# The last ten pairs of heads of an attention stage, taken four heads at a time: chunks of 128 keys and one 64x64-tile step for the keys left over

## The chip, the core and the metric

The kernel runs on one core of a Trainium2 chip. TensorE (PE) multiplies, VectorE (DVE), ScalarE (ACT) and GpSimd (POOL) do the elementwise work, and SyncE (SP) issues nearly all DMAs. The metric is the device time of one execution in microseconds (us), as the median of several runs; less is better.

## What is computed

Three stages in fp32. Sigmoid attention for 4 batches of 12 heads (448 keys and queries, head size 64), a gated product with w_a, w_b and w_out on its 1792 rows, and a soft mixture of 8 experts:

```python
def _attn_ref(q, k, v):                      # (4, 12, 448, 64)
    scores = scale * np.matmul(q, k.transpose(0, 1, 3, 2)) - np.log(S)
    attn = 1.0 / (1.0 + np.exp(-scores))
    return np.matmul(attn, v)

x = attn_out.transpose(0, 2, 1, 3).reshape(B * S, H * D)
x = (x @ w_a) * (x @ w_b) @ w_out            # 768 -> 1536 -> 768
logits = x @ phi                             # 32 slots, softmax over tokens and over slots
slot_out[e] = np.maximum(slot_input[e] @ w1[e], 0) @ w2[e]
out = c @ slot_out
```

## The kernel before

The attention goes by pairs of heads, numbered g = 0 to 23 (six pairs in a batch, the two heads of a pair on partitions 0 to 63 and 64 to 127). For one pair:

- `load_qkv` loads k and q as four DMAs each and v as one DMA, all on SP's queue. For pairs 13 to 23 k and q arrive in blocks of 32 that VectorE transposes in place (`transposed`), and `split_heads` makes a rounded fp32r part (`kh`, `qh`) and a rest (`kl`, `ql`) of each. Two buffers hold each of these, three each of the loads.
- `emit_S` makes the scores in four chunks of 112 keys. A chunk is three fp32r products (kh·qh, kl·qh, kh·ql) for each head; the two heads have different rows of the array and run side by side. ScalarE's sigmoid takes each chunk of 112x448 from PSUM to a tile `a`.
- `emit_PV` multiplies the `a` tiles with v in full fp32: four chunks, the two heads in different columns of the array, side by side, both into one PSUM tile. `emit_x` copies that on ScalarE to the tile that the next stage reads, frees v, and asks for the v of the pair three further on.

`att` is a generator that fixes the order. In the step of pair g, from pair 12 on, it writes: transposes and split of pair g+1; the first chunk of scores of g; PV and x of pair g-1; the other chunks of g. The caller takes a step of it and then a step of other work: `operands` and `prep_u`, which prepare the next stage (POOL subtractions, rounding casts `S2h` and `wx` on VectorE that wait for POOL), and the group and logits work of batch 0 (`first_LG`). After the last scores the first product of `unit(0)` (banks `ab`) is issued, then PV and x of pair 23, then the rest of `unit(0)`, which goes on with `late_operands` that need the last x.

A load waits on SP for its buffer, and whatever stands behind it on SP waits too. PSUM has tags `sc` (4 buffers), `ms` (2) and `ab` (2). The end of the kernel streams the experts' weights through buffers that come free as earlier stages end.

Of the kernel before, what the change touches and what calls it, by code (L numbers as in the profile page):

```python
# [9 lines left out]
F32 = mybir.dt.float32  # L10
# [25 lines left out]
def body(ctx, tc, q, k, v, w_a, w_b, w_out, phi, w1, w2, out):  # L36
# [81 lines left out]
    qkv_t = {}  # L118
    held = []

    def load_qkv(g, names):
# [6 lines left out]
        for src, nm, n in ((k, "k", 3), (q, "q", 3), (v, "v", 3)):  # L128
            if nm not in names:
                continue  # L130

            if g >= GT0:
                if nm == "v":
                    t = atp.tile([T, 2, C, D], F32, tag="vn", name="vn", bufs=n)
                    sp.dma_start(out=t, in_=src[b, 2 * p:2 * p + 2].rearrange("h (c p) d -> p h c d", c=C))
                else:
                    t = atp.tile([128, 2 * C * D], F32, tag=nm + "n", name=nm + "n", bufs=n)
                    t = t[:, :S].rearrange("p (n d) -> p n d", d=32)
                    for j in range(4):
                        sp.dma_start(out=t[32 * j:32 * j + 32],  # L140
                                     in_=src[b, 2 * p + j // 2][:, j % 2 * 32:j % 2 * 32 + 32].rearrange(
                                         "(n t) d -> t n d", t=32))
                qkv_t[nm, g] = t
                continue
            s = src[b, 2 * p:2 * p + 2].rearrange(
                "h (c p) d -> p h c d" if nm == "q" else "h (p c) d -> p h c d", c=C)
            if nm == "v":
                t = atp.tile([T, 2, C, D], F32, tag="vn", name="vn", bufs=n)
                sp.dma_start(out=t, in_=s)
            else:  # L150
                t = atp.tile([128, 2 * C * D], F32, tag=nm + "n", name=nm + "n", bufs=n)
# [5 lines left out]
    stk = {}  # L157
# [21 lines left out]
    def emit_TK(g):  # L179
        if g >= B * NP:  # L180
            return
        if g >= GT0:
            for nm in "kq":
                split_heads(g, nm, transposed(g, nm), dve.tensor_copy)
                load_qkv(g + 3, nm)
            return
        tk = transposed(g, "k")
        if not g:
            tq = transposed(g, "q")
        split_heads(g, "k", tk, dve.tensor_copy)  # L190
        if not g:
            split_heads(g, "q", tq, act.copy)
# [8 lines left out]
    def emit_S(g, chunks):  # L201

        (kh, kl), (qh, ql) = stk[g]["k"], stk[g]["q"]
        for c in chunks:
            ab = (g < NP or g > 2 * NP) and c == 2
            sc = [ms((T, S)) if g >= GT0 and c == 0 and not h else ps_tile("ab" if ab else "sc", [T, S], 2 if ab else 4)
                  for h in range(2)]
            cs = slice(c * T, (c + 1) * T)
            for i, (kx, qx) in enumerate(((kh, qh), (kl, qh), (kh, ql))):
                for h in range(2):  # L210
                    r = slice(64 * h, 64 * h + 64)
                    pe.matmul(sc[h], kx[r, cs], qx[r], start=(i == 0), stop=(i == 2))  # L212
            for h in range(2):
                a = atp.tile([T, S], F32, tag="a", name="a", bufs=11)
                act.activation(a, sc[h], AF.Sigmoid, bias=nlog[:T], scale=1.0 / math.sqrt(D))  # L215
                a_t[g, h, c] = a

    pv_t = {}

    def emit_PV(g, cs):  # L220
        if cs[0] == 0:
            pv_t[g] = ps_tile("sc", [128, S], 4) if g < 2 * NP else ms()
        for c in cs:
            for h in range(2):
                pe.matmul(pv_t[g][64 * h:64 * h + 64], qkv_t["v", g][:, h, c, :], a_t.pop((g, h, c)),  # L225
                          start=(c == 0), stop=(c == C - 1))

    xt = {}

# [12 lines left out]
    def emit_x(g):  # L242
        pv = pv_t.pop(g)
        qkv_t.pop(("v", g))
        b, kk = divmod(g, NP)
        if b:
            xt[g] = raw_x(b, kk)
            act.copy(xt[g], pv)
        else:
            xh = x0p.tile([128, S], F32R, tag=f"xh{kk}", name=f"xh{kk}")  # L250
            xl = x0p.tile([128, S], F32R, tag=f"xl{kk}", name=f"xl{kk}")
            act.activation(xh, pv, AF.Copy)
            dve.tensor_tensor(xl, pv, xh.bitcast(F32), op=ALU.subtract)
            xt[g] = (xh, xl)
        load_qkv(g + 3, "v")

    def att():
# [483 lines left out]
    def unit(u):  # L741
# [520 lines left out]
```

## Time and profile before

| | |
|---|---|
| median of 3 runs (lowest to highest) | 674.41 us (674.21 to 678.49) |
| the profiled execution | 674.89 us, its span 673.1 us |
| TensorE busy | 635.7 us, 94% |
| VectorE, ScalarE, POOL busy | 390.6, 290.8, 309.5 us |
| TensorE's granted clock, mean | 0.989 of full speed |

The span runs from the first instruction to the last; the 1.8 us around it belong to the time as well. Busy shares are averages over stages with different limits. Pairs 14 to 23 lie between 226 and 292 us of the span.

### The profile page before, as it was taken

How to read it: one execution, taken by the hardware profiler on the slowest of the kernel's cores; microseconds unless marked ns; L12 is line 12 of the kernel's file. 1: busy time of each engine (PE TensorE's matmuls, PEld its weight loads, DVE VectorE, ACT ScalarE, POOL GpSimd, SP SyncE). 2: the span in 40 equal slices, each digit the busy share in tenths (PEclk: the TensorE clock that was granted, in tenths of full speed). 3: DMA queues.
4: the chain of work that ended last, by engine and by line, in shares of the span. 5: the costliest groups of instructions: out<-in, count | busy, mean ns of one | idle time of the engine just before them, and what ended most of it. 6: DMA issues, size and time to landing. Idle time of an engine off the chain costs nothing.

```text
span 673.1 us, 10911 instructions
## 1 busy us (share of the span) xinstructions
PE 635.7 (94%) x4035; PEld 451.7 (67%) x4035; DVE 390.6 (58%) x563; ACT 290.8 (43%) x527; POOL 309.5 (46%) x236
## 2 busy tenths in 40 slices
PE   6999999999998899999999999999999998997685
PEld 4456777777765455569989898898879896442131
DVE  4675898999973769657876777754233322200013
ACT  4888778779645588763432223201110002110022
POOL 0233677686745239558996585742344442000000
PEclk9999999999999999999999999999999999999788
DMA  9997999998868977201123233341999999999998
GB/s 211 272 247 215 288 291 335 287 296 265 259 151 203 247 126 134 64 2 47 48 89 95 70 93 99 97 126 44 305 384 344 407 357 339 405 415 416 411 374 307
DMA packets 150356, 154.25 MB, mean 229 GB/s; under 512 B 81856, under 2 KB 126752, under 8 KB 147232
## 3 DMA queue, kind: packets, MB, share of 16 engines
q1 hardware_dynamic: 143728, 150.00, 71.9%
q10 hardware_dynamic: 6576, 3.56, 1.8%
q8 instruction: 32, 0.52, 0.3%
q14 instruction: 20, 0.16, 0.1%
HBM read 126.36 MB, written 27.17 MB: 228 GB/s over the span
## 4 chain that ended last, share of the span: by engine, by line
PE 80%; DMA 12%; ACT 2%; DVE 2%; SPq 1%; issue 1%; ACTq 1%; POOL 0%; POOLq 0%; DVEq 0%
PE ab L578 26%; PE sc L761 15%; DMA e<-in_moe_w 8%; PE ab L761 8%; PE sc L212 7%; PE sc L225 5%; PE ms L225 5%; PE ms L174 2%; PE ms L854 2%; PE ab L212 2%; DMA gkp<-in_moe_w 1%; PE ms L501 1%; PE ms L400 1%; PE ms L212 1%; SPq L140 1%
## 5 line engine op out<-in xcount | busy, mean ns | idle before, releaser
L375 POOL TENSOR_TENSOR w<-gk,cy 128x768 int32<-128x768 int32 x36 | 66.1, 1837 | 91.7 <-DVE gk L370 53.7
L215 ACT ACTIVATE a<-sc,sums 112x448 f32<-112x448 f32 x147 | 84.3, 642 | 14.2 <-PE sc L212 14.1
L578 PE MATMUL ab<-t,wh 128*128 128x448 f32 x288 | 65.1, 371 | 0.0
L578 PEld LDWEIGHTS ab<-t,wh 128*128 128x128 f32 x288 | 53.4, 188 | 6.1 <-issue 1.3
L471 POOL TENSOR_TENSOR wl<-wr,wh 128x768 fp32r<-128x768 f32 x16 | 29.5, 1841 | 49.8 <-DVE wh L470 26.0
L585 ACT COPY misc<-ab 128x448 f32<-128x448 f32 x24 | 12.9, 537 | 83.3 <-PE ab L578 76.4
L471 POOL TENSOR_TENSOR wl<-w,wh 128x768 fp32r<-128x768 f32 x24 | 46.6, 1942 | 2.5 <-ACT wh L470 2.5
L1188 PE MATMUL ab<-e,gk 128*32 128x384 f32 x240 | 33.6, 567 | 10.1 <-DMA e<-in_moe_w 10.1
L588 DVE TENSOR_TENSOR misc<-misc,ab 128x448 f32<-128x448 f32 x24 | 14.7, 614 | 44.1 <-PE ab L578 44.1
L225 PE MATMUL sc<-a,vn 112*64 112x448 f32 x192 | 39.1, 546 | 1.0 <-ACT a L215 1.0
L225 PE MATMUL ms<-a,vn 112*64 112x448 f32 x192 | 38.7, 546 | 1.1 <-ACT a L215 1.1
L368 DVE TENSOR_SCALAR mf<-gk 128x768 f32<-128x768 f32 x36 | 33.8, 940 | 8.3 <-ACT gk L357 8.3
L212 PE MATMUL sc<-qh,kh 64*112 64x448 f32 x147 | 34.5, 421 | 0.7 <-ACT qh L162 0.6
L578 PE MATMUL ab<-xh,wl 128*128 128x448 f32 x144 | 34.3, 374 | 0.9 <-POOL wl L471 0.9
L369 DVE TENSOR_SCALAR gk<-mf 128x768 uint32<-128x768 uint32 x36 | 34.3, 953 | 1.2
L578 PE MATMUL ab<-xh,wh 128*128 128x448 f32 x144 | 34.9, 378 | 0.0
L641 ACT CAST wx<-T 128x384 fp32r<-128x384 f32 x21 | 10.8, 513 | 55.6 <-DVE T L663 40.0
L578 PE MATMUL ab<-xl,wh 128*128 128x448 f32 x144 | 34.5, 375 | 0.0
L642 POOL TENSOR_TENSOR wx<-wr,wx 128x384 fp32r<-128x384 f32 x29 | 32.8, 1133 | 3.5 <-ACT wx L641 3.4
L578 PE MATMUL ab<-t,wl 128*128 128x448 f32 x144 | 34.3, 373 | 0.0
L642 POOL TENSOR_TENSOR wx<-T,wx 128x384 fp32r<-128x384 f32 x23 | 24.6, 1068 | 19.8 <-ACT wx L641 18.5
L1235 DVE COPY o<-sc 128x384 f32<-128x384 f32 x10 | 5.4, 555 | 48.0 <-PE sc L1214 46.8
(465 smaller groups left out, 1494.5 us busy)
## 6 DMA issues: line engine op xcount, KB each, us to landing
e<-in_moe_w SPq DMA_DIRECT2D x23, 1024.0 KB, 8.4
e<-in_moe_w SPq DMA_DIRECT2D x23, 768.0 KB, 15.0
wr<-ab SPq DMA_DIRECT2D x14, 768.0 KB, 4.5
ab<-w SPq DMA_DIRECT2D x24, 384.0 KB, 7.1
vn<-in_v SPq DMA_DIRECT2D x24, 224.0 KB, 4.5
gk<-gk SPq DMA_DIRECT2D x24, 224.0 KB, 4.2
e<-in_moe_w SPq DMA_DIRECT2D x14, 384.0 KB, 8.8
wr_cv<-in_moe_w_a SPq DMA_DIRECT2D x6, 768.0 KB, 6.5
```

The lines of the kernel that those rows point to most:

```text
L212: pe.matmul(sc[h], kx[r, cs], qx[r], start=(i == 0), stop=(i == 2))
L215: act.activation(a, sc[h], AF.Sigmoid, bias=nlog[:T], scale=1.0 / math.sqrt(D))
L225: pe.matmul(pv_t[g][64 * h:64 * h + 64], qkv_t["v", g][:, h, c, :], a_t.pop((g, h, c)), start=(c == 0), stop=(c == C - 1))
L368: dve.tensor_scalar(mf, m, LOW, HIGH, op0=ALU.max, op1=ALU.min)
L369: dve.tensor_scalar(mi, mf.bitcast(U32), 3, 0x3FFFFFFF, op0=ALU.logical_shift_left, op1=ALU.bitwise_and)
L375: pool.tensor_tensor(thirds(w), m.bitcast(I32), thirds(cy_t.pop(x)), op=ALU.add)
L471: pool.tensor_tensor(wl, t, wh.bitcast(F32), op=ALU.subtract)
L578: pe.matmul(t, w[:, kk * 128:(kk + 1) * 128], xt[b * NP + kk][xi], start=(s == 0 and kk == 0), stop=(s == 2 and kk == KD - 1))
L588: dve.tensor_tensor(g, g, t, op=ALU.mult)
L642: pool.tensor_tensor(w[:, 1], t, w[:, 0].bitcast(F32), op=ALU.subtract)
L761: pe.matmul(t, w[:, wi, k * 128:(k + 1) * 128], xs[ORDER[m], k][xi], start=(s == 0 and k == 0), stop=(s == 2 and k == 2))
L1188: pe.matmul(sps[h][32 * j:32 * j + 32], hT[:, 2 * x + i, 2 * j + g], ring[order2[n + j]][0][:, i, c0:c0 + w], start=(g == 0 and x == 0 and ...
```

## The change

From pair 14 on (`GQ`) two pairs make a group of four heads n to n+3: the even pair holds heads n and n+3, the odd pair n+2 and n+1. Each pair does three chunks of 128 keys. The 64 keys that are left of each of the four heads are done once per group, at the odd pair: `emit_S_rest` has four fp32 products of 64 rows by 64 columns, one in each quarter of the array, and two sigmoids of 128x448; the odd pair's PV ends with four such products of 64x64 more. PV of a group goes to two `ab` tiles, and both x copies come after the odd pair's PV, one on ScalarE and one on VectorE. q stays in its buffer until `emit_S_rest` (four buffers), and the 64 k columns are copied to `kr`. v comes in four DMAs instead of one. The first product of `unit(0)` and the logits of batch 0 use other banks, and one step of `rest_LG` is later.

The diff, without what only moves lines:

```diff
+GQ = 2 * NP + 2
+    def heads(g):
+        n = 2 * (g % NP)
+        return (n, n + 1) if g < GQ else (n, n + 3) if g % 2 == 0 else (n, n - 1)
...
+                else:
+                    t = t.rearrange("p (c d) -> p c d", d=D)
+                    for h in range(2):
+                        sp.dma_start(out=t[:, 3 * h:3 * h + 3],
+                                     in_=src[b, hs[h]][:384].rearrange("(c p) d -> p c d", c=3))
+                    rest = (hs[0], hs[0] + 2) if g % 2 == 0 else (hs[1], hs[1] + 2)
+                    for h in range(2):
+                        sp.dma_start(out=t[64 * h:64 * h + 64, 6], in_=src[b, rest[h]][384:])
...
-                split_heads(g, nm, transposed(g, nm), dve.tensor_copy)
-                load_qkv(g + 3, nm)
+                t = transposed(g, nm)
+                split_heads(g, nm, t, dve.tensor_copy)
+                if g >= GQ:
+                    if nm == "k":
+                        kr = atp.tile([128, 64], F32, tag="kr", name="kr", bufs=3)
+                        dve.tensor_copy(kr, t[:, 384:])
+                        t = kr
+                    whole[nm, g] = t
+                if nm == "k" or g <= GQ:
+                    load_qkv(g + 3, nm)
...
+    def emit_S_rest(g):
+        sc = [ms() for _ in range(2)]
+        for d in range(2):
+            for h in range(2):
+                r, f = slice(64 * h, 64 * h + 64), 64 * (d ^ h)
+                pe.matmul(sc[h][f:f + 64], whole["k", g - 1 + d][r], whole["q", g - 1 + d][r], start=True, stop=True)
+        for h in range(2):
+            sigmoid(g, h, 3, sc[h], 128)
+        for d in range(2):
+            del whole["k", g - 1 + d], whole["q", g - 1 + d]
+            load_qkv(g + 3 + d, "q")
...
+        for c in range(3):
+            for h in range(2):
+                pe.matmul(pv[h ^ odd][64 * h:64 * h + 64], qkv_t["v", g][:, 3 * h + c], a_t.pop((g, h, c)),
+                          start=(c == 0), stop=False)
+        if odd:
+            a = [a_t.pop((g, h, 3)) for h in range(2)]
+            for r in range(2):
+                for h in range(2):
+                    s = slice(64 * r, 64 * r + 64)
+                    pe.matmul(pv[r][64 * h:64 * h + 64], qkv_t["v", g - 1 + h][s, 6], a[h][s], start=False, stop=True)
...
-            act.copy(xt[g], pv)
+            (dve.tensor_copy if g > GQ and g % 2 else act.copy)(xt[g], pv)
...
-                emit_PV(g - 1, (0, 1, 2, 3))
-                emit_x(g - 1)
+                emit_PV(g - 1)
+                if g <= GQ:
+                    emit_x(g - 1)
+                elif g % 2 == 0:
+                    emit_x(g - 2)
+                    emit_x(g - 1)
...
+                if g >= GQ and g % 2:
+                    emit_S_rest(g)
+                    yield 800
...
-            tag = UBANK[(7 * u + m) % 6]
+            tag = UBANK[(7 * u + m) % 6] if u + m else "sc"
...
-        lf = ms()
+        lf = ms() if b else ps_tile("ab", [128, S], 2)
...
-        for _ in range(4 if b == 1 else 1):
+        for _ in range((3, 4, 1)[b]):
```

Where it moves instructions. On TensorE, before, the last chunk of scores of pair 15 and the PV of pair 14 (names as in the code, `x8` for eight instructions in a row):

```order
L212 MATMUL ms<-qh,kh 112x448
L212 MATMUL sc<-qh,kh 112x448
L212 MATMUL ms<-qh,kl 112x448
L212 MATMUL sc<-qh,kl 112x448
L212 MATMUL ms<-ql,kh 112x448
L212 MATMUL sc<-ql,kh 112x448
L225 MATMUL ms<-a,vn 64x448 x8
```

On TensorE now, from the left-over scores of pairs 14 and 15 over the first chunk of pair 16 to the PV of pair 15 and the left-over PV:

```order
L253 MATMUL ms<-qn,kr 64x448 x4
L238 MATMUL sc<-qh,kh 128x448 x2
L238 MATMUL sc<-qh,kl 128x448 x2
L238 MATMUL sc<-ql,kh 128x448 x2
L277 MATMUL ab<-a,vn 64x448 x6
L284 MATMUL ab<-a,vn 64x448 x4
```

Eight products of PV are six, and the two steps of four stand at the odd pair alone. On SP's queue, before, the loads of pairs 17 (k, q), 15 (v), 18 (k, q), 16 (v) and 19 (k, q), with a store of logits among them:

```order
L140 DMA kn_2518<-in_k 32x14x32 x4
L140 DMA qn_2528<-in_q 32x14x32 x4
L135 DMA vn_2569<-in_v 112x8x64
L140 DMA kn_2634<-in_k 32x14x32 x4
L140 DMA qn_2644<-in_q 32x14x32 x4
L135 DMA vn_2678<-in_v 112x8x64
L867 DMA clog32_101<-ls_d_2454 448x1x32
L140 DMA kn_2728<-in_k 32x14x32 x4
L140 DMA qn_2738<-in_q 32x14x32 x4
```

On SP's queue now, from the v of pair 15: k of 18, v of 16, the store, k of 19, q of 18 and of 19, k of 20, v of 17 (two rows a v):

```order
L155 DMA vn_2574<-in_v 128x3x64 x2
L159 DMA vn_2574<-in_v 64x64 x2
L146 DMA kn_2644<-in_k 32x14x32 x4
L155 DMA vn_2683<-in_v 128x3x64 x2
L159 DMA vn_2683<-in_v 64x64 x2
L932 DMA clog32_101<-ls_d_2457 448x1x32
L146 DMA kn_2726<-in_k 32x14x32 x4
L146 DMA qn_2790<-in_q 32x14x32 x4
L146 DMA qn_2795<-in_q 32x14x32 x4
L146 DMA kn_2807<-in_k 32x14x32 x4
L155 DMA vn_2841<-in_v 128x3x64 x2
```

The q of two pairs go together behind `emit_S_rest`, the v of two pairs together behind the odd pair's PV, and v of 17 has moved behind q of 18, q of 19 and k of 20. On VectorE, before, from the third `S2h` cast, which waits for POOL, to the k of pair 21:

```order
L669 CAST S2h_3086<-s_3038 128x448
L641 CAST wx_3106<-wr 128x384
L170 STREAM_TRANSPOSE kn<-kn 128x448
L162 CAST kh<-kn 128x448
L163 TENSOR_TENSOR kl<-kn,kh 128x448
```

On VectorE now, from the end of pair 21's split over the same cast to the k of pair 22:

```order
L186 STREAM_TRANSPOSE qn<-qn 128x448
L178 CAST qh<-qn 128x448
L179 TENSOR_TENSOR ql<-qn,qh 128x448
L734 CAST S2h_3147<-s_3099 128x448
L706 CAST wx_3167<-wr 128x384
L306 COPY t_3187<-ab 128x448
L186 STREAM_TRANSPOSE kn<-kn 128x448
L178 CAST kh<-kn 128x448
L179 TENSOR_TENSOR kl<-kn,kh 128x448
L205 COPY kr<-kn 128x64
```

The copy of x and the copy to `kr` are new there, and five `wx` casts that stood ahead of pair 23 now stand behind it.

## Rows read from the trace of the kernel before

**Rows 1.** The page, the chain that ended last: shares of the span by engine.

```profile
PE 80%; DMA 12%; ACT 2%; DVE 2%; SPq 1%; issue 1%; ACTq 1%; POOL 0%; POOLq 0%; DVEq 0%
```

**Rows 2.** Stretches of the span: length, busy time by engine, clock, DMA share, GB/s.

```profile
core 0: us, PE busy (x) PEld busy (x) DVE busy (x) ACT busy (x) POOL busy (x), PEclk, DMA share, GB/s
237.00:242.75 5.75, 5.75 (x44) 3.07 (x42) 3.15 (x6) 4.84 (x9) 0.00 (x0) 1.00 0.74 130
254.25:260.00 5.75, 5.75 (x42) 3.07 (x40) 5.58 (x7) 4.84 (x9) 4.80 (x5) 1.00 0.74 122
300.00:455.00 155.00, 155.00 (x772) 138.96 (x771) 111.95 (x161) 43.16 (x95) 109.93 (x99) 1.00 0.30 83
480.00:560.00 80.00, 80.00 (x553) 68.05 (x553) 24.92 (x45) 6.46 (x14) 32.37 (x18) 1.00 1.02 362
```

**Rows 3.** Timeline of TensorE, one pair: start, length, line, operation, count.

```profile
242.75 0.46 PE L212 MATMUL sc<-qh,kh 64*112 64x448 f32 x2
243.04 0.36 PE L212 MATMUL sc<-qh,kl 64*112 64x448 f32 x2
...
245.34 3.23 PE L225 MATMUL ms<-a,vn 112*64 112x448 f32 x16
248.50 0.46 PE L212 MATMUL sc<-qh,kh 64*112 64x448 f32 x2
```

**Rows 4.** Timeline of TensorE, products with 128 columns of weights, in the next stage.

```profile
298.93 0.77 PE L761 MATMUL sc<-A12l,wx 128*128 128x448 f32 x3
299.54 0.57 PE L761 MATMUL sc<-A12h,wx 128*128 128x448 f32 x2
```

**Rows 5.** Timeline of TensorE near the end: four fp32 products of 32x64, 384 columns.

```profile
655.75 0.88 PE L1214 MATMUL sc<-gk,misc 32*64 32x384 f32 x8
656.56 1.81 PE L1188 MATMUL ab<-e,gk 128*32 128x384 f32 x19
```

**Rows 6.** Timeline of TensorE, where the attention begins and ends; wait in brackets.

```profile
221.66 0.66 PE L540 MATMUL ms<-ident,misc 128*128 128x128 f32 x4 [1.42 <-DVE ls_d L819]
...
231.20 0.46 PE L212 MATMUL sc<-qh,kh 64*112 64x448 f32 x2
...
288.44 3.23 PE L225 MATMUL ms<-a,vn 112*64 112x448 f32 x16
...
294.78 3.50 PE L854 MATMUL ms<-gk,ls_d 128*32 128x128 f32 x96 [0.72 <-ACT S1h L669]
```

**Rows 7.** Timeline of SP's queue: start and length of DMA issues.

```profile
232.92 0.42 SPq L135 DMA_DIRECT2D vn<-in_v  x1
...
239.16 0.63 SPq L867 DMA_DIRECT2D clog<-ls_d  x1
239.88 2.13 SPq L140 DMA_DIRECT2D kn<-in_k  x4
242.11 1.99 SPq L140 DMA_DIRECT2D qn<-in_q  x4
244.22 0.41 SPq L135 DMA_DIRECT2D vn<-in_v  x1
```

**Rows 8.** DMA issues from 195 to 290 us: count, size, median us to landing.

```profile
vn<-in_v SPq DMA_DIRECT2D x11, 224.0 KB, 3.5
...
qn<-in_q SPq DMA_DIRECT2D x36, 56.0 KB, 2.4
```

**Rows 9.** The weight loads of the last stage, one line: shortest, median, longest issue in ns.

```profile
L1003 SPq DMA_DIRECT2D e<-in_moe_w x46: 327/328/583, 498.7 to 625.2; - x46
```

**Rows 10.** Timeline of VectorE beside POOL's work: subtractions, and a wait for POOL.

```profile
251.31 1.45 DVE L163 TENSOR_TENSOR kl<-kn,kh 128x448 fp32r<-128x448 f32 x1
...
262.55 0.39 DVE L669 CAST S2h<-s 128x448 fp32r<-128x448 f32 x1 [1.05 <-POOL s L689]
```

**Rows 11.** Timeline of ScalarE and VectorE: one x copy, one VectorE copy from PSUM.

```profile
248.64 0.54 ACT L248 COPY misc<-ms 128x448 f32<-128x448 f32 x1 [0.64 <-PE ms L225]
...
220.99 0.61 DVE L819 COPY ls_d<-ms 128x448 f32<-128x448 f32 x1
```

More of the change, by code (lines that the diff above doesn't have):

```diff
@@ L119, in body, with chunks_of @@
     held = []
+    def heads(g):
+        n = 2 * (g % NP)
+        return (n, n + 1) if g < GQ else (n, n + 3) if g % 2 == 0 else (n, n - 1)
+    def chunks_of(g):
+        return (T, C) if g < GQ else (128, 3)
     def load_qkv(g, names):
@@ L127, in load_qkv @@
         b, p = divmod(g, NP)
-        for src, nm, n in ((k, "k", 3), (q, "q", 3), (v, "v", 3)):
+        for src, nm, n in ((k, "k", 3), (q, "q", 4), (v, "v", 3)):
             if nm not in names:
                 continue
+            t = atp.tile([128, 2 * C * D], F32, tag=nm + "n", name=nm + "n", bufs=n)
             if g >= GT0:
[L133 to L137, printed above, removed]
+                hs = heads(g)
+                if nm != "v":
                     t = t[:, :S].rearrange("p (n d) -> p n d", d=32)
@@ L147, in load_qkv @@
             if nm == "v":
-                t = atp.tile([T, 2, C, D], F32, tag="vn", name="vn", bufs=n)
+                t = t[:T].rearrange("p (h c d) -> p h c d", h=2, c=C)
                 sp.dma_start(out=t, in_=s)
             else:
-                t = atp.tile([128, 2 * C * D], F32, tag=nm + "n", name=nm + "n", bufs=n)
                 t = t[:T].rearrange("p (c h d) -> p c h d", c=C, h=2)
@@ L155, in load_qkv @@
             qkv_t[nm, g] = t
-    stk = {}
+    stk, whole = {}, {}
     def split_heads(g, nm, t, rnd):
@@ L203, in emit_S @@
         (kh, kl), (qh, ql) = stk[g]["k"], stk[g]["q"]
+        n, _ = chunks_of(g)
         for c in chunks:
-            ab = (g < NP or g > 2 * NP) and c == 2
-            sc = [ms((T, S)) if g >= GT0 and c == 0 and not h else ps_tile("ab" if ab else "sc", [T, S], 2 if ab else 4)
+            ab = (g < NP or 2 * NP < g < GQ) and c == 2
+            by_ms = c == 0 and (g % 2 if g >= GQ else g >= GT0)
+            sc = [ms((n, S)) if by_ms and (g >= GQ or not h) else ps_tile("ab" if ab else "sc", [n, S], 2 if ab else 4)
                   for h in range(2)]
-            cs = slice(c * T, (c + 1) * T)
+            cs = slice(c * n, (c + 1) * n)
             for i, (kx, qx) in enumerate(((kh, qh), (kl, qh), (kh, ql))):
@@ L213, in emit_S @@
             for h in range(2):
-                a = atp.tile([T, S], F32, tag="a", name="a", bufs=11)
-                act.activation(a, sc[h], AF.Sigmoid, bias=nlog[:T], scale=1.0 / math.sqrt(D))
-                a_t[g, h, c] = a
-    pv_t = {}
[L220 to L223, printed above, removed]
-            for h in range(2):
-                pe.matmul(pv_t[g][64 * h:64 * h + 64], qkv_t["v", g][:, h, c, :], a_t.pop((g, h, c)),
-                          start=(c == 0), stop=(c == C - 1))
+                sigmoid(g, h, c, sc[h], n)
@@ new lines, in sigmoid @@
+    def sigmoid(g, h, c, sc, n):
+        a = atp.tile([128, S], F32, tag="a", name="a", bufs=11)[:n]
+        act.activation(a, sc, AF.Sigmoid, bias=nlog[:n], scale=1.0 / math.sqrt(D))
+        a_t[g, h, c] = a
+    def emit_S_rest(g):
[9 more added lines that the diff above has]
+            load_qkv(g + 3 + d, "q")
@@ new lines, in body, with emit_PV @@
+    pv_t = {}
+    def emit_PV(g):
+        if g < GQ:
+            pv = pv_t[g] = ps_tile("sc", [128, S], 4) if g < 2 * NP else ms()
+            for c in range(C):
+                for h in range(2):
+                    pe.matmul(pv[64 * h:64 * h + 64], qkv_t["v", g][:, h, c, :], a_t.pop((g, h, c)),
+                              start=(c == 0), stop=(c == C - 1))
+            return
+        odd = g % 2
+        if not odd:
+            for d in range(2):
+                pv_t[g + d] = ps_tile("ab", [128, S], 2)
+        pv = pv_t[g - odd], pv_t[g - odd + 1]
+        for c in range(3):
+            for h in range(2):
+                pe.matmul(pv[h ^ odd][64 * h:64 * h + 64], qkv_t["v", g][:, 3 * h + c], a_t.pop((g, h, c)),
[6 more added lines that the diff above has]
+                    pe.matmul(pv[r][64 * h:64 * h + 64], qkv_t["v", g - 1 + h][s, 6], a[h][s], start=False, stop=True)
@@ L263, in att @@
             dense = g < NP or g >= 2 * NP
-            first = ((0, 1) if g == 0 else (0, 2) if g == B * NP - 1 else (0,) if dense else ()) if more else ()
+            first = ((0, 1) if g in (0, B * NP - 1) else (0,) if dense else ()) if more else ()
             if g:
@@ L294, in att @@
                     yield 430
-                for c in range(C):
+                for c in range(chunks_of(g)[1]):
                     if c not in first:
```

5 lines of the change are left out of this document (4 added, 1 removed).

## The prediction

> **What bounds the kernel now.** I read the chain that ended last first: TensorE holds 80% of it [rows 1]. Then the stretches: from pair 16 on TensorE is busy all the time at full clock, ScalarE for 4.84 of 5.75 us, VectorE for 3.15 us of a pair where POOL rests and 5.58 us where POOL works [rows 2]. So the stretch that the change touches is bound by TensorE, and VectorE stands close behind it. What is won there reaches the end: TensorE is full from 300 to 455 us, and from 480 us on the DMAs are (share 1.02) [rows 2]; these read weights into buffers that come free with the work ahead, so they begin earlier by what the attention wins. The timeline of one pair gives the prices: 5.75 us from its second chunk of scores to that of the next, 2.59 us of it for twelve steps of scores, 3.16 us from the first product of PV to the next scores [rows 3]. A step after PV takes 0.29 us [rows 3], other steps 0.20 (2.59 less 0.29, over eleven, with 0.1 left for the way into PV): a change of tiles costs about 0.1 us.
>
> **TensorE's sum.** A chunk of 128 keys has the same 448 columns as one of 112. That its weights are wider need not cost: with 128 columns of weights three steps take 0.61 us, 0.203 each [rows 4]. So a pair's scores go from 2.59 to 1.98 us (one chunk of 0.61 less), and its PV from 3.16 to three chunks of 0.79, 2.37 us. Two steps of four 64x64 products per group are new. No row shows fp32 in quarters of the array at 448 columns. Bound from below: all four in the time of one chunk of PV, 0.79. From above: one after another, four times that, 3.2. The nearest row has four fp32 products of 32x64 (rows and columns of the array both apart) with 384 columns in 0.81 us [rows 5]; one after another they would take more than twice that, since two of PV side by side take 0.79 with 448 columns. I take 0.85, scaled by little for the columns. Three more changes of tiles in a group add 0.1 each. A group: 2 x 1.98 + 6 x 0.79 + 2 x 0.85 + 0.3 = 10.7 us, before 11.5. Five groups win 4.0 us.
>
> Absolute times: after the PV of pair 13 the scores of 14 went on at 231.20 [rows 6]; with two chunks of 0.61 and a change of tiles instead of three, pair 15 would begin at 232.5. With 5.34 us for an odd pair's step and 5.36 for an even one's the PV of 15, 17, 19 and 21 would begin at 238.7, 249.4, 260.1 and 270.8. From there to the PV of 23: PV of 21 (3.3), the rest of 22 (1.3), pair 23 (5.4), the first product of `unit(0)` (2.2): 12.2 us, so 283.0, where before it began at 288.44 [rows 6]. That is 5.4 us (four from the groups, the rest because nothing waits there, and pair 23 has a chunk less). After it TensorE waited 0.72 us for a cast [rows 6]; the step that waited now stands two products of `unit(0)` later, so that 0.7 goes too: 6.1 us if nothing is late.
>
> The logits' other bank takes away a wait of up to 1.42 us at 221.66 [rows 6]. The three more DMAs of pair 14's v, ahead of the group stores on SP, put those up to 1.4 us later. I let these two cancel.
>
> **What is late: v.** Before, v took one issue; k and q four each. From one issue to the next: k 2.23 us, q 2.11, v 0.5, the logits store 0.72 [rows 7]. Now v takes four. None of that size is in the trace: from below 0.33 + 0.1 of gap each [rows 9], 1.7 in all; from above 0.5 each, 2.0. I take 1.9. So k, q and v of a group need 2 x (2.2 + 2.1 + 1.9) = 12.4 us of SP, and TensorE would take 10.7. Before it was 9.7 of 11.5. The queue, not the bytes, is the limit: DMA share 0.74 over a pair [rows 2].
>
> From 232.92 (v of 15 [rows 7]; before that SP is held by the loads of `wr`, same now) the order is v15, k18, v16, store, k19, q18, q19, k20, v17: 1.9 + 2.2 + 1.9 + 0.7 + 2.2 + 4.2 + 2.2 = 15.3, so v17 begins at 248.2. Its second piece, for the second head, is issued 0.5 later and lands after 2.4 us (pieces of 56 KB) to 3.5 (224 KB) [rows 8]; for 96 KB I take 3.0: 251.7. PV of 17 could begin at 249.4. It waits 2.3 us, and behind it on TensorE stand the scores of 18 and all that follows. v19: 12.4 us of issues later, landed at 264.1; PV of 19 could begin at 251.7 + 10.7 = 262.4 and waits 1.7. v21: 10.2 us later (no k or q of 24), landed at 274.3; PV of 21 would begin at 274.8, so no wait. With 12.2 to the PV of 23: 287.0. That is 1.4 us before 288.44, and 2.1 with the 0.7 behind it, less 0.1 for its left-over products: 2.0.
>
> On the two pieces of 64 keys the Trainium skill (DMA: Bandwidth & Descriptors, Rules for kernel authors) advises against this change: "Two transfers to disjoint partition halves: Don't bother — they serialize", one transfer being better. By that rule the split buys nothing and adds an issue; the sum charges just that. No run here shows the pieces yet.
>
> **Beside the path.** ScalarE loses two sigmoids of sixteen and one copy of two in a group: 4.84 x 2 less three times some 0.54 [rows 2, 11], about 8.1 of 10.7 us: hidden. VectorE gains a copy from PSUM per group (0.61 [rows 11]) and two to `kr`, a seventh of a tile each, below 0.2: 0.5 us a pair. At 3.15 that hides. Where POOL works (a subtraction of 1.45 us [rows 10]) a pair takes 5.6 + 0.5 = 6.1 against 5.35: cover gone. But POOL's subtractions now come in two lots, after the x of 15 and after those of 16 and 17, and while PV waits for v VectorE catches up. One place stays: the third `S2h` cast stands ahead of pair 22's split and waited 1.05 us for POOL [rows 10]; I bound what it holds up between 0 and 1.5 us and take 0. The five `wx` casts behind pair 23 now have the last PV to hide behind.
>
> **The sum.** Against the profiled execution 674.89 - 2.0 = 672.9; against the median, 0.5 lower, 672.4.
>
> **Rivals.**
> - *The loads keep up.* If an issue of v costs little, or SP gets ahead while the first pairs run, nothing waits: 674.4 - 6.1 = 668.3, and 666.9 if the 1.42 us at 221.66 goes too. For: before, v17 was issued at 244.2 [rows 7], 5 us before PV needs it now. Against: four issues of v and a q and k more in front of it. v17 now has the buffer of 14, free only after PV of 15. The Trainium skill (DMA: Bandwidth & Descriptors, Rules for kernel authors) says to issue early and wait late, so that the fixed setup overlaps; by that rule this rival holds where the buffer is free early enough.
> - *The quarters don't run four at once* (the other side). Each of the ten steps would take 1.6 (two at once) or 3.2 (one after another). Two at once adds 7.5 us to the group sum; then a group takes 12.2, SP keeps up, and it ends at 668.3 + 7.5 = 675.8. One after another: 668.3 + 23.5 = 691.8. It is slower than before from a price of 0.85 + 0.61 = 1.46 us a step. Against: [rows 5].
> - *VectorE is the bound.* With 6.1 us for five pairs, 18 to 22, it loses 5 x 0.75 = 3.8 of 6.1: 672.1; on top of some of v's lateness up to 676. For: 5.58 us with POOL at work [rows 2].
>
> **Numbers.** v late: 0.60, its own range 669.5 (1.7 us a v, landing 2.4) to 675.0 (SP 1.4 later, 2.0 a v, `S2h` 1.5). Loads keep up: 0.18. Quarters: 0.10, half of it above 680. VectorE: 0.12. The predicted time is that of the first, 672.4 us. The range 667.0 to 677.0 leaves out the slow half of the quarters and the best of the loads. A measurement of this kernel can tell about 1% from no change: faster is below 667.7, slower above 681.2. Faster: most of the chance that the early wait goes too or the steps are cheaper than I took, 0.13. Slower: one after another, or several waits at once, 0.06. Same: 0.81.
>
> **What would show it.** A step of scores with 128 keys at 0.20, a step of four in 0.8 to 0.95, a group's work without waits at 10.7. PV of 17 waiting some 2 us for a DMA of v, that of 19 less; SP issuing without a pause from 233 to 275. The last PV beginning at 287. I am wrong on the term that decides if PV waits for no DMA, or if the waits there are for VectorE or for scores.

## The result and the profile after

The changed kernel takes 678.2 us (median of 22 runs, 674.9 to 680.3), the kernel before 672.95 (22 runs, 671.2 to 678.5). The ratio is 1.0069, with a 95% interval of 1.0054 to 1.0084: 0.7% slower, some 4.6 us. The prediction was 672.4 with a range of 667.0 to 677.0 and a small gain: the number is outside the range and the sign is wrong. The prediction had counted from 674.41 us, the median of the first three runs of before; with 22 runs before takes 1.5 us less. Against before it promised a gain of 2.0 us, and the medians show a loss of 5.3: the 5.8 us between 672.4 and 678.2 understate the miss.

The profiled execution of the changed kernel took 677.31 us (span 675.5), that of before 674.89 (span 673.1). Before's lies 1.9 us above its median and after's 0.9 below, so this pair shows 2.4 of the 5 us. The trace of after also lies 0.3 to 0.9 us earlier where no edit reaches, ahead of pair 13. I therefore count from the PV of pair 12, which starts at 217.02 before and at 216.16 after, to the PV of pair 23: 71.42 us before, 75.81 after.

The chain that ended last, from the page of after, the counterpart of [rows 1]; SP's queue has gone from 1% to 3%, TensorE from 80% to 78%:

```profile
PE 78%; DMA 13%; SPq 3%; DVE 2%; ACT 2%; issue 1%; ACTq 0%; POOL 0%; DVEq 0%; POOLq 0%
```

Stretches of the changed kernel, columns as in [rows 2]; where TensorE was busy all the time in pairs 16 to 18 before, it now has holes, and its granted clock falls:

```profile
237.00:260.00 23.00, 18.67 (x110) 8.76 (x112) 12.63 (x20) 10.83 (x21) 6.85 (x6) 0.85 0.56 99
245.00:250.00 5.00, 3.35 (x28) 1.66 (x26) 1.79 (x4) 3.37 (x7) 0.00 (x0) 1.00 0.66 107
250.00:255.00 5.00, 2.54 (x8) 1.06 (x9) 4.83 (x7) 1.16 (x2) 3.83 (x3) 0.52 0.56 113
255.00:260.00 5.00, 5.00 (x31) 2.35 (x29) 1.92 (x4) 0.97 (x2) 0.61 (x1) 0.80 0.49 84
```

TensorE's timeline of the changed kernel (L277 is PV by chunks of 128 keys, L284 the left-over PV, L238 scores, L253 left-over scores):

```profile
237.23 2.81 PE L277 MATMUL ab<-a,vn 128*64 128x448 f32 x12 [0.66 <-DMA vn<-in_v]
...
241.59 0.37 PE L238 MATMUL sc<-qh,kh 64*128 64x448 f32 x2
241.79 0.36 PE L238 MATMUL sc<-qh,kl 64*128 64x448 f32 x2
...
246.72 0.98 PE L253 MATMUL ms<-qn,kr 64*64 64x448 f32 x8
249.35 0.47 PE L238 MATMUL sc<-qh,kh 64*128 64x448 f32 x2 [1.65 <-DVE qh L178]
252.95 4.79 PE L277 MATMUL ab<-a,vn 128*64 128x448 f32 x12 [2.46 <-DMA vn<-in_v]
257.67 0.98 PE L284 MATMUL ab<-a,vn 64*64 64x448 f32 x8
267.14 2.85 PE L277 MATMUL ab<-a,vn 128*64 128x448 f32 x12 [0.90 <-DMA vn<-in_v]
272.85 2.48 PE L277 MATMUL ab<-a,vn 128*64 128x448 f32 x12
279.10 0.47 PE L238 MATMUL sc<-ql,kh 64*128 64x448 f32 x2 [0.58 <-DVE ql L179]
279.50 2.48 PE L277 MATMUL ab<-a,vn 128*64 128x448 f32 x12
291.97 2.48 PE L277 MATMUL ab<-a,vn 128*64 128x448 f32 x12
```

VectorE of the changed kernel: a transpose of q that waits for its load, a copy to `kr` where POOL rests, and two where POOL works:

```profile
244.67 0.18 DVE L205 COPY kr<-kn 128x64 f32<-128x64 f32 x1
248.14 0.65 DVE L186 STREAM_TRANSPOSE qn<-qn 128x448 f32<-128x448 f32 x1 [3.29 <-DMA qn<-in_q]
267.20 1.12 DVE L205 COPY kr<-kn 128x64 f32<-128x64 f32 x1
275.41 1.00 DVE L205 COPY kr<-kn 128x64 f32<-128x64 f32 x1
```

These rows show four kinds of loss. PV waits for v at 15, 17 and 19. The scores of 18 wait 1.65 us for `qh`; VectorE had itself waited 3.29 us for the load of q. PV of 17 takes 4.79 us where PV of 23 takes 2.48: the granted clock is 0.52 from 250 to 255 us, which is nearly all at the level of 1.2 GHz. And from PV of 20 to PV of 21 it is 6.65 us (279.50 less 272.85), where PV of 14 to PV of 15 is 5.53 in the run without late loads below; the scores of 22 wait for VectorE there.

SP's queue of the changed kernel, as in [rows 7] (L146 k and q, L155 the 384 keys of v, L159 the left-over keys):

```profile
221.98 1.03 SPq L694 DMA_DIRECT2D wr<-ab  x2
223.05 4.78 SPq L146 DMA_DIRECT2D kn<-in_k  x4
227.88 6.51 SPq L146 DMA_DIRECT2D qn<-in_q  x4
234.50 0.95 SPq L155 DMA_DIRECT2D vn<-in_v  x2
235.49 1.13 SPq L159 DMA_DIRECT2D vn<-in_v  x2
...
244.13 4.07 SPq L146 DMA_DIRECT2D qn<-in_q  x8
248.30 1.99 SPq L146 DMA_DIRECT2D kn<-in_k  x4
250.39 0.95 SPq L155 DMA_DIRECT2D vn<-in_v  x2
251.69 1.12 SPq L159 DMA_DIRECT2D vn<-in_v  x2
...
264.27 0.96 SPq L155 DMA_DIRECT2D vn<-in_v  x2
```

SP issues almost without a pause from 223 to 280 us. From v17 (250.39) to v19 (264.27) it needs 13.9 us for a group. Behind the loads of `wr` the eight issues of k17 and q17 take 11.3 us, where eight issues of q take 4.07 later: single issues are held there for up to 3.06 us (3.68 in the kernel before).

### The profile page after: what moved, and what is told of

Same layout as the page of the kernel before. It is cut to its first block, busy times and chain, and to the rows that moved or that the text cites. A ratio compares the mean times of both kernels' runs of the same rounds, so it can differ in the third digit from the quotient of the medians.

```text
span 675.5 us, 10900 instructions
## 1 busy us (share of the span) xinstructions
PE 636.1 (94%) x4015; PEld 448.3 (66%) x4015; DVE 401.8 (59%) x578; ACT 283.6 (42%) x512; POOL 308.5 (46%) x236
## 4 chain that ended last, share of the span: by engine, by line
PE 78%; DMA 13%; SPq 3%; DVE 2%; ACT 2%; issue 1%; ACTq 0%; POOL 0%; DVEq 0%; POOLq 0%
PE ab L643 26%; PE sc L826 16%; DMA e<-in_moe_w 8%; PE ab L826 7%; PE sc L238 6%; PE sc L267 5%; PE ab L277 3%; PE ms L190 2%; PE ms L919 2%; DMA qn<-in_q 1%; DMA gkp<-in_moe_w 1%; SPq L146 1%; PE ms L566 1%; DMA vn<-in_v 1%; SPq L622 1%
## 5 line engine op out<-in xcount | busy, mean ns | idle before, releaser
L244 ACT ACTIVATE a<-sc,sums 112x448 f32<-112x448 f32 (+1 forms) x147 | 82.5, 638 | 19.6 <-PE sc L238 19.3
L238 PE MATMUL sc<-qh,kh 64*112 64x448 f32 (+1 forms) x147 | 33.6, 429 | 2.6 <-DVE qh L178 1.8
L277 PE MATMUL ab<-a,vn 128*64 128x448 f32 x120 | 27.8, 581 | 4.0 <-DMA vn<-in_v 4.0
```

Of the source, the lines that this page charges most:

```text
L244: act.activation(a, sc, AF.Sigmoid, bias=nlog[:n], scale=1.0 / math.sqrt(D))
L277: pe.matmul(pv[h ^ odd][64 * h:64 * h + 64], qkv_t["v", g][:, 3 * h + c], a_t.pop((g, h, c)), start=(c == 0), stop=False)
```

## The experiments

Theory A: what counts is the number of DMA issues on SP's queue, so loads come late. Rivals: B, the transfers themselves (small pieces, bytes); C, VectorE beside POOL. All ratios are against before, run in turn on the same chip; the medians are of five groups of runs, in which before took 672.95 to 673.76. `e1_v_one` and `e8_all_one` load rows in another order, so that their outputs are not the reference's. The fourth column is taken from the profiled execution of each kernel, from the start of PV of 12 to that of PV of 23; one execution need not lie at the median (that of `f4_wr_in_gap` was the slowest of its twelve).

| kernel | us, median | ratio and 95% interval | PV 12 to PV 23 |
|---|---|---|---|
| before | 672.95 | 1 | 71.42 |
| after | 678.20 | 1.0069 (1.0054 to 1.0084) | 75.81 |
| `e1_v_one` | 671.89 | 0.9957 (0.9932 to 0.9981) | 70.77 |
| `e2_wr_late` | 677.70 | 1.0060 (1.0036 to 1.0084) | 75.28 |
| `e3_before_v4` | 678.79 | 1.0078 (1.0052 to 1.0104) | 76.73 |
| `e4_fill` | 679.93 | 1.0073 (1.0050 to 1.0096) | 79.12 |
| `e5_v_act` | 692.49 | 1.0283 (1.0255 to 1.0311) | 91.27 |
| `e6_v_two` | 674.88 | 1.0026 (1.0006 to 1.0046) | 73.17 |
| `e8_all_one` | 667.45 | 0.9920 (0.9898 to 0.9942) | 67.95 |
| `e9_v_two_act` | 684.53 | 1.0177 (1.0144 to 1.0210) | 83.19 |
| `f1_two_late` | 670.54 | 0.9952 (0.9932 to 0.9972) | 68.66 |
| `f2_two_late_act` | 678.57 | 1.0067 (1.0040 to 1.0094) | 75.07 |
| `f3_k_like_q` | 670.56 | 0.9959 (0.9942 to 0.9977) | 68.35 |
| `f4_wr_in_gap` | 669.61 | 0.9925 (0.9900 to 0.9950) | 69.62 |

### One issue for v

```diff
-                    for h in range(2):
-                        sp.dma_start(out=t[:, 3 * h:3 * h + 3], in_=src[b, hs[h]][:384]...)
-                    rest = ...
-                    for h in range(2):
-                        sp.dma_start(out=t[64 * h:64 * h + 64, 6], in_=src[b, rest[h]][384:])
+                    sp.dma_start(out=t[:, :7], in_=src[b, 2 * p:2 * p + 2].rearrange("h s d -> (h s) d").rearrange(
+                        "(c p) d -> p c d", c=7))
```

> The changed kernel with v of the pairs from 14 on in one DMA issue each instead of four: the same bytes, the same number of 256-byte pieces on 128 partitions, but rows of v in another order, so the output is not the reference's. Theory A (SP issues too many DMAs): each v costs SP 0.5 us instead of 2.2, so v15 and v16 give back some 3.4 us, v17 goes out near 247 instead of 250.4, the wait for q of 18 (1.65 us) goes, PV of 17 waits 1 us or less and its 4.8 us fall to 2.5; time 670 to 672, 6 to 8 us below the changed kernel's 678.2. Theory B (the bytes or small pieces fill the DMA engines): nothing goes earlier, PV of 17 still waits over 2 us, 677 to 679. Theory C (VectorE is the bound): no change, 677 to 679.

Measured: 671.89 us, 6.3 under after, as A expects. Bytes and pieces are the same, so B falls. SP's queue and TensorE of this kernel:

```profile
245.20 1.03 SPq L154 DMA_DIRECT2D vn<-in_v  x2
```

```profile
236.56 2.48 PE L273 MATMUL ab<-a,vn 128*64 128x448 f32 x12 [1.58 <-DMA vn<-in_v]
248.64 2.48 PE L273 MATMUL ab<-a,vn 128*64 128x448 f32 x12 [1.12 <-DMA vn<-in_v]
259.70 2.48 PE L273 MATMUL ab<-a,vn 128*64 128x448 f32 x12
```

The v of 17 and 18 go out in 1.03 us at 245.20, 5.2 us earlier than after's, or 3.6 counted from PV of 12. The wait for q of 18 is gone. PV of 15 still waits 1.58 us, PV of 17 waits 1.12 us and runs at full clock, PV of 19 waits for nothing.

### Four issues for v in the kernel before

```diff
-                    sp.dma_start(out=t, in_=src[b, 2 * p:2 * p + 2].rearrange("h (c p) d -> p h c d", c=C))
+                    for j in range(4):     # pairs from 14 on
+                        h, i = j // 2, j % 2
+                        sp.dma_start(out=t[:, h, 2 * i:2 * i + 2],
+                                     in_=src[b, 2 * p + h][224 * i:224 * i + 224].rearrange("(c p) d -> p c d", c=2))
```

> The kernel before with one part of the change alone: v of the pairs from 14 on in four DMA issues (56 KB each) instead of one; the tiles of 112 keys and all products stay. Theory A (the issues on SP are the loss): SP needs 2.2 + 2.1 + 2.0 = 6.3 us per pair against TensorE's 5.75, and v17 goes out some 4.5 us later, at 248.7 with its landing at 251.5 against a need at 251.1: small waits for v or q from pair 17 on, 674 to 677 against 673.0 before. Theory B (the loss comes with the new tiles or with VectorE): no wait, 672.5 to 673.5.

Measured: 678.79 us, slower than I expected of A (674 to 677) and much slower than B's no change. The issues alone, with the old tiles, cost as much as the whole change. SP needs 6.2 us for k, q and v of a pair (from v at 260.19 to the next v at 266.36), TensorE 5.75 [rows 3]:

```profile
260.19 1.92 SPq L140 DMA_DIRECT2D vn<-in_v  x4
262.21 1.97 SPq L146 DMA_DIRECT2D kn<-in_k  x4
264.28 1.99 SPq L146 DMA_DIRECT2D qn<-in_q  x4
266.36 1.92 SPq L140 DMA_DIRECT2D vn<-in_v  x4
```

The waits of TensorE for v add up to 2.4 us, at PV of 18 (two of them) and of 21. PV of 17 and 21 took 4.05 and 4.23 us instead of 3.23, at full clock. That they held on inside for a piece of v is inferred from the length and not shown.

### All loads in one issue: the ceiling

```diff
-                    for j in range(4):
-                        sp.dma_start(out=t[32 * j:32 * j + 32], in_=...)
+                    sp.dma_start(out=t, in_=src2.rearrange("(n t) d -> t n d", t=128))   # k and q; v as in e1_v_one
```

> The changed kernel with k, q and v of the pairs from 14 on in one DMA issue each instead of four: same bytes and pieces of the same size (128 bytes for k and q, 256 for v), but in another order, so the output is not the reference's. SP then needs some 3 us a group. Theory A (the sum of the prediction for nothing late, 6.1 us below before): no wait for a load from pair 16 on, PV of 23 some 5 to 6 us sooner after PV of 12 than before, 667 to 668.5. Theory B (VectorE is next in line, with its casts and subtractions beside POOL in pairs 18 to 22): waits for qh and ql of 1 to 4 us appear instead, 669 to 672. Theory C (small pieces fill the DMA engines): waits for DMAs of k and q stay, 672 or more.

Measured: 667.45 us, at the bottom of A's numbers. No load is waited for; what is left are two waits for VectorE, 1.2 us together, of the kind that B of this run named, so both were partly right:

```profile
PE sc L238 <- DVE qh L178: 0.6, 1, 0.6
PE sc L238 <- DVE ql L179: 0.6, 1, 0.6
```

Its groups are 10.88 us (PV of 15 at 234.59, 17 at 245.47, 19 at 256.35), then 13.38 to 21 (269.73): that group is 2.5 us longer, of which the two waits name 1.2. Small pieces do not fill the DMA engines: theory C of this run falls.

### Keeping TensorE busy while it waits

```diff
+    def filler(g, n):
+        (kh, _), (qh, _) = stk[g]["k"], stk[g]["q"]
+        for _ in range(n):
+            pe.matmul(pv_t[17][:64], kh[:64, :64], qh[:64], start=True, stop=True)
...
+            if g == 18:
+                filler(17, 9)      # ahead of the scores of 18; filler(18, 13) behind their first chunk
```

> The changed kernel with 22 spare 64x64 products on TensorE (9 ahead of the scores of 18, 13 ahead of PV of 17, into a half of a bank that PV of 17 starts afresh), only to keep TensorE busy while it waits there for q and v. They compute nothing that is used. Theory A (the idle time costs twice: the granted clock is 0.50 from 250.6 to 257, and PV of 17 takes 4.79 us instead of 2.48 for that reason): the clock stays at 1.00, PV of 17 takes 2.5 us from nearly the same start, and all that follows is some 2 to 2.5 us earlier where loads allow: 675.5 to 677 against 678.2. Theory B (PV of 17 takes 4.79 because the later pieces of v land one after another): it keeps that length and the time stays 678 to 680.

Measured: 679.93 us, no gain. TensorE and the clock in this run:

```profile
238.87 4.36 PE L282 MATMUL ab<-a,vn 128*64 128x448 f32 x12 [2.19 <-DMA vn<-in_v]
256.18 3.00 PE L282 MATMUL ab<-a,vn 128*64 128x448 f32 x12
269.76 4.39 PE L282 MATMUL ab<-a,vn 128*64 128x448 f32 x12 [2.10 <-DMA vn<-in_v]
```

```profile
240.00:245.00 5.00, 5.00 (x25) 1.77 (x23) 0.87 (x3) 0.53 (x1) 0.00 (x0) 0.66 0.53 98
255.00:260.00 5.00, 5.00 (x27) 2.08 (x25) 2.87 (x5) 0.00 (x0) 1.24 (x1) 1.00 0.35 78
270.00:275.00 5.00, 5.00 (x20) 1.56 (x18) 4.18 (x6) 0.00 (x0) 4.06 (x4) 0.66 0.47 89
```

On the mechanism A was right: where the spare products stand, the clock stays at 1.00 and PV of 17 takes 3.00 us. Unfilled waits of 2.19 and 2.10 us, at 15 and 19, are followed by PVs of 4.36 and 4.39 us. On the time A was wrong: v19 is issued 14.5 us after v17 (267.12 and 252.61), in after 13.9, and PV of 19 waits 2.10 us where after's waited 0.90. Part of that is the execution: v15 went out 1.9 us later than in after, ahead of any spare product, and PV of 15 waited 2.19 us instead of 0.66. What the medians say is that nothing is won: with the queue setting the pace, TensorE got its time back as a wait.

### An earlier start, and half of the issues

```diff
-    load_u(0)
-    load_u(1)
+    nu = 0
     for cost in att_g:
+        while nu < 2 and ("v", 18 + 2 * nu) in qkv_t:
+            load_u(nu)
+            nu += 1
```

> The changed kernel with one thing moved: the two loads of wr for the next stage (768 KB each), issued at 222 us ahead of k17, q17 and v15, are issued behind v18 and v20. Theory A (SP's queue is behind when the groups begin, because k17, q17 and v15 stand behind wr for 11 us): v15 goes out 6 to 8 us earlier, near 227, no product of scores or PV waits for k, q or v, the clock stays whole, and the time is what I had reckoned for nothing late, 668 to 671. Theory B (the rate alone counts, 12.4 us of issues per group against 10.7): the head start is used up within four groups, one or two waits stay at 19 and 21, 672 to 675. Theory C (wr is needed early, or VectorE behind POOL is the bound): new waits for casts of wr or the same time as before, 676 or more.

Measured: 677.70 us, nothing won. v15 does go out 4.3 us earlier (230.18; 5.3 counted from PV of 12), less than I had said, and PV of 15 waits for nothing. PV of 17 already waits 1.08 us, and at 19 the lead is gone (the first row is the scores of 20, the second PV of 19):

```profile
262.82 0.47 PE L238 MATMUL sc<-qh,kh 64*128 64x448 f32 x2 [2.81 <-DVE qh L178]
266.05 5.06 PE L277 MATMUL ab<-a,vn 128*64 128x448 f32 x12 [2.19 <-DMA vn<-in_v]
```

From v17 (246.97) to v19 (263.17) SP needed 16.2 us here, a load of `wr` among them. This is Theory B of this run in its mechanism, with a worse time than I gave it. The time lies where I had put Theory C, but no product waits for a cast of `wr`, and PV of 20 to PV of 21 takes 5.54 us, so VectorE is not what holds it. PV of 19 takes 5.06 us, at a granted clock of 0.50.

The other half of the test is the rate, with v in half of the issues:

```diff
+                    sp.dma_start(out=t[:, :6].rearrange("p (h c) d -> p h (c d)", h=2),
+                                 in_=hp[:, :384].rearrange("h (p c) d -> p h (c d)", c=3))
+                    for r in range(0 if odd else 2):
+                        sp.dma_start(out=t[64 * r:64 * r + 64, 6:8],
+                                     in_=src[b, n + 2 * r:n + 2 * r + 2, 384:].rearrange("h p d -> p h d"))
...
+            cs = slice(c * n, (c + 1) * n) if g < GQ else slice(c, 384, 3)
```

> The changed kernel with the same v in half of the issues, result unchanged: the two heads' 384 keys in one issue (keys dealt to the chunks in threes, 768-byte pieces, the key columns of k read with a step of three to match), and the left-over keys of all four heads in two issues per group, with the first v of the group. A group has 4 issues for v instead of 8. Theory A (the count of issues on SP): SP needs about 13.3 - 2.4 = 10.9 us a group, as much as TensorE, so what is late at 15 stays late by about as much, and 17, 19 are late by no more than in the run with one issue per v: 671.5 to 674. Rival: the step of three in the weight loads costs time of its own: TensorE's scores take over 0.25 us a step, and the time stays at 676 or more.

Measured: 674.88 us, a little above the range I gave. One wait for v is left, 2.79 us at 17, longer than the run with one issue per v had there, and PV of 17 takes 3.71 us after it. VectorE holds up pair 21 as in `e8_all_one` (7.75 us from PV of 20 to PV of 21). The step of three in the weight loads is cheap: PV of 15 to PV of 16 takes 5.42 us, with one issue per load 5.34. Start and rate together:

> The changed kernel with v in half of the issues (four in a group) and the two loads of wr behind v18 and v22 instead of ahead of k17; result unchanged, all on SP. Theory A (queue: both its start and its rate count; the late wr alone did nothing because 13.3 us of issues a group ate the lead, half of the issues alone left one wait of 2.8 us at 17 because the start was late): v17 goes out near 244.5, no wait of TensorE for a DMA anywhere, clock whole, only the waits for VectorE of about 1.2 us at pair 21 stay as in the run with one issue per load: 667.5 to 669.5. Rival: wr comes too late for the casts on VectorE, or its 768 KB delay the loads behind it: waits for q, k or wx, 672 or more.

Measured: 670.54 us, 7.7 under after and 0.5% faster than before; that is a little above A's 667.5 to 669.5 and below the rival's. The waits of TensorE in this kernel from pair 14 on, as totals by line:

```profile
PE ab L278 <- DMA vn<-in_v: 0.7, 1, 0.7
PE sc L239 <- DVE ql L180: 0.5, 1, 0.5
PE sc L239 <- ACT a L245: 0.3, 1, 0.3
```

A holds in the main: either edit alone leaves the queue behind, both together bring it nearly level. The wait for v, at 19, is one that A had excluded; the load of `wr` now stands ahead of that v.

### ScalarE's queue

```diff
-                        sp.dma_start(...)
+                        act.dma_start(...)     # the four issues of v from pair 14 on
```

> The changed kernel with the four DMA issues of each v from pair 14 on moved from SP's queue to ScalarE's; sizes and count as they are. Theory A (SP's queue is what is late): SP is left with 8.5 us of issues for a group's k and q against TensorE's 10.9, so no product waits for q, and the v are issued as soon as their buffer is free. If an issue holds ScalarE as long as it holds SP (some 0.55 us), ScalarE needs 8.1 + 4.5 = 12.6 us a group and becomes the bound: waits for sigmoids instead, 672 to 676; if it holds ScalarE for 0.1 us or less, 667 to 670. Theory B (the transfers themselves are slow, whoever issues them): waits for v as before, 677 to 679.

Measured: 692.49 us, far from anything I expected. TensorE waits 13.7 us once, for `qh` of 17, because q17 was issued at 252.60. What held SP longest, from its queue's waits, and ScalarE's queue in the same run:

```profile
SPq L622 <- DMA vn<-in_v: 12.9, 1, 12.9
```

```profile
223.55 0.53 ACT L306 COPY r<-ms 128x448 f32<-128x448 f32 x1 [2.52 <-issue]
223.58 0.91 ACTq L155 DMA_DIRECT2D vn<-in_v  x2
224.53 1.16 ACTq L159 DMA_DIRECT2D vn<-in_v  x2
```

The trace of this run shows eight completion counters (semaphores) for all DMAs, each used by DMAs of both engines, 56 or 57 times in all; they go round in the order of the program, and a DMA waits for the earlier one on its counter. SP's group stores (L622) waited for v15, whose issue stands on ScalarE behind an x copy and came at 223.58. The theory on SP's load was not refuted by that, but this run cannot test it. An issue holds ScalarE as long as SP: 0.91 us for two. `e9_v_two_act` has the same fault with half of the issues:

> The kernel with v in half of the issues (four in a group, result unchanged), and these issues on ScalarE's queue instead of SP's. Theory A: SP has 8.5 us of issues a group, ScalarE 8.1 + 4 x 0.55 = 10.3 at most, both below TensorE's 10.9: only the wait at pair 15 can stay, the rest of the sum of the prediction for nothing late is had: 667.5 to 670, under both kernels. Theory B (ScalarE's queue blocks behind a v whose buffer is not free, and sigmoids behind it): waits of TensorE for sigmoids, 671 to 675.

Measured: 684.53 us, above both ranges, with a wait of 8.4 us for `qh` of 17. The theories on ScalarE's time could not be told apart for the same reason. `f2_two_late_act`, with only the large issue from pair 17 on moved, is the rival's case:

> The kernel of f1_two_late with the one large issue of each v from pair 17 on put on ScalarE's queue. The 8 completion counters are shared by the two queues in program order, so SP also waits for what ScalarE issued. Theory A: at pairs 17 and later ScalarE is never far behind, so SP gains 0.5 us a pair that it no longer needs: within 0.3% of f1_two_late. Rival (the coupling costs whenever ScalarE waits for TensorE): 671 or more, with waits for q.

Measured: 678.57 us, 8.0 above `f1_two_late`, with 2.2 us of waiting for `qh` of 20.

### What VectorE adds, and the version that is left

```diff
-                    if nm == "k":
-                        kr = atp.tile([128, 64], F32, tag="kr", name="kr", bufs=3)
-                        dve.tensor_copy(kr, t[:, 384:])
-                        t = kr
                     whole[nm, g] = t
-                if nm == "k" or g <= GQ:
+                if g <= GQ:
                     load_qkv(g + 3, nm)
```

> The kernel of f1_two_late, with k kept whole until the left-over scores like q (four buffers, ten instead of eleven buffers for the sigmoids), so that VectorE's two copies to kr per group fall away, and k19 and k20 are issued with q, v17 ahead of k20. Theory (VectorE is what is left: the copies to kr take 1.0 to 1.1 us each beside POOL): the 1.2 us of waits for VectorE at pair 21 go, 666.5 to 668.5, 0.5 to 1.2 us under f1_two_late. Rival (k issued later, or ten buffers for the sigmoids are too few): new waits for k or of ScalarE, 668.5 or more.

Measured: 670.56 us, no better than `f1_two_late`. In place the theory holds: no wait for VectorE is left, and from PV of 20 to PV of 21 it is 5.91 us, 6.95 in `f1_two_late` and 7.79 in `e8_all_one`. The gain was lost ahead of that, at PV of 19, which waits 1.66 us for v (0.73 in `f1_two_late`) and starts 0.7 us later counted from PV of 12. With k asked for behind `emit_S_rest` too, SP's queue stood empty from 231.2 to 235.5 us, and v17 and v19 went out 0.9 and 0.6 us later, counted in the same way. So the rival's time came, by a wait for v and not for k.

> The kernel of f3_k_like_q with the first load of wr moved from behind v18 (246.4 us) to behind v16, where SP's queue stood empty from 231.2 to 235.5 us in that run; result unchanged. Theory (the wait of 1.66 us at PV of 19 is the queue held up for 3 us behind the 768 KB of wr among the loads of 20): that wait goes and nothing new comes, 668 to 670, 1 to 2 us under f3_k_like_q. Rival (wr at 231 us only holds up k18, q18 and v17 instead): a wait at 17 or for q of 18, 670 to 673.

Measured: 669.61 us, ratio 0.9925: the fastest version with an unchanged result, but its intervals overlap those of `f1_two_late` and `f3_k_like_q`. Its theory falls: the wait at 19 stays and one at 21 comes, with `wr` far away. What stands ahead of v19 is sixteen issues of k and q, as in `f1_two_late`, and ahead of v21 as many; that these are the cause was not tested:

```profile
260.64 2.48 PE L274 MATMUL ab<-a,vn 128*64 128x448 f32 x12 [1.56 <-DMA vn<-in_v]
273.36 2.48 PE L274 MATMUL ab<-a,vn 128*64 128x448 f32 x12 [1.53 <-DMA vn<-in_v]
```

After these waits PV takes 2.48 us. Neither filled waits nor k and q in fewer issues with the right order were tried in this version.

## Why the prediction was wrong

**TensorE's sum was right.** Scores of 128 keys take 0.20 us a step, a step of four 64x64 products 0.91 to the next start (I took 0.85), three chunks of PV 2.41 (2.37). A group where nothing is late takes 10.88 us, I had 10.7. So the four products do run at once. The rival for "loads keep up" gave 668.3, and `e8_all_one` took 667.45; that agreement is in part luck. It promised 6.1 us under before, and `e8_all_one` was 5.6 under it in its own runs: TensorE's early wait gave more and VectorE took more than I had counted.

**What is late: right in kind, too small in size.** The step that failed is "What is late: v", by the sizes of its terms: the queue was the limit, as I had said, but it was further behind. Beside it failed "Beside the path", which put VectorE at nothing.

| | predicted | after |
|---|---|---|
| v15 issued | 232.9 | 234.50 |
| v17 issued | 248.2 | 250.39 |
| PV of 17 starts | 251.7 | 252.95 |
| v17 to v19 on SP | 12.4 | 13.88 |
| PV of 19 starts | 264.1 | 267.14 |
| PV of 21 starts | 274.8 | 279.50 |
| PV of 23 starts | 287.0 | 291.97 |

The predicted times are on the axis of before's trace; after's lies 0.7 to 0.9 us earlier, so the true lateness is that much more than the differences here. Four terms make the 5 us at the end:

- *An issue of v.* I took 1.9 us, at most 2.0. With four equal pieces that is what it costs (1.92 in `e3_before_v4`). But the two pieces of 64 keys take 1.13 us together and the two of 384 keys 0.95, and with the gaps v17 and v18 hold SP for 4.86 us, 2.43 each; that is 1.1 of the 1.5 us by which the group is longer than I said (the rest is one k, held for 2.67). The row on weight loads [rows 9] was the wrong neighbour. The Trainium skill (DMA: Bandwidth & Descriptors, Rules for kernel authors) says that two transfers to disjoint partition halves serialize and that one should be used. The trace shows this of the issues, 0.56 us for each 16 KB half, one behind the other; that the transfers themselves serialize no run here shows. A whole v in one issue took 0.37 to 0.51 us in `e1_v_one`.
- *"I let these two cancel."* The logits' other bank did take the early wait away (PV of 12 to PV of 13: 9.08 us, before 10.69), and SP did come later, as v14's three more DMAs would make it: v15 went out 1.6 us after my 232.9. They do not cancel, because they fall on different sides of the race: TensorE came sooner to a v that came later.
- *What else hangs on the queue.* I priced v alone. q of 18, issued behind it, held the scores of 18 for 1.65 us, and with the two waits the granted clock fell (0.50 while PV of 17 waited) and PV of 17 took 2.3 us more, 1.8 of it by the clock if `e4_fill` is the measure (3.00 us at full clock). The prediction had no term for the clock. `e4_fill` shows that the end does not pay this term on top: v19 was as late as that anyway.
- *VectorE.* I took the two copies to `kr` as "below 0.2". Seven of ten take 0.18 to 0.19 us, but the three beside POOL take 1.00 to 1.12. From PV of 20 to PV of 21 TensorE needs 7.79 us in `e8_all_one`, where no load is late, against 5.53 from PV of 14 to PV of 15. In after it needs 6.65: VectorE did catch up while PV waited, as I had said, and 1.1 us stayed. Without the copies it is 5.91 (`f3_k_like_q`; 6.95 in `f1_two_late`). I had put this on the rival "VectorE is the bound" alone, as if one of the two had to be it. It came on top of the late v. The `S2h` cast, which I had bounded at 1.5, was not the cause: it had no wait in after.

**The end.** The wait of 0.72 us behind PV of 23 is gone, as predicted.

What stays open: profiles and medians differ. The profiled pair shows 2.4 us, the medians 5.3, and I did not find which part of the run varies from run to run by these few us. One place is on record: the eight issues of k17 and q17 take 11.3 us in the profiled execution of after and 12.4 in that of `e4_fill`, which is the same kernel up to there.

## What to carry to other kernels

Count DMA instructions per unit of work for each queue, with the price of each kind of piece from the trace, and set the sum against the engine that is to be made faster: here a gain of 0.6 us in the 11.5 of a group was lost to six more issues at half a microsecond each. When a queue is the pace setter, price everything that stands in it, not only the load that the change touches; speeding up the waiting engine yielded nothing here (`e4_fill`). Delays from two causes add when they lie at different pairs; giving each a chance of its own as rivals hides their sum.

## What the runs showed of the hardware

- A DMA issue of k, q or v held SP for a median of 0.42 us with 224 KB (before), 0.48 with 56 KB, 0.49 with 96 KB and 0.56 with 16 KB on 64 partitions (after); on ScalarE two of 96 KB took 0.91 us, two of 16 KB 1.16. Behind the 768 KB loads of `wr` single issues of k and q took up to 3.06 us.
- A copy of 128x64 on VectorE took 0.18 us, and 1.00 to 1.12 beside subtractions on POOL.
- Four fp32 products of 64x64 in the quarters of the array, with 448 columns, took 0.91 us to the next start; a chunk of two products of 128x64 took 0.80.
- After a wait of TensorE of 1.66 us (`f3_k_like_q`) PV took 2.48 us; after waits of 2.10 and 2.19 (`e4_fill`) it took 4.39 and 4.36, with a granted clock of 0.66 over the 5 us around it.
- Moving DMA issues to another engine's queue made SP wait up to 12.9 us for a DMA that stood on ScalarE, through the completion counters that the two queues share; TensorE waited 13.7 us at one place.
